# Routed attention and a gated layer on one core: later planned landings, a re-searched order, and code copies on GpSimd

## Chip, cores and metric

The kernel runs on one core of a Trainium2 chip. The metric is the device time of one execution in microseconds (us); the median of three runs of the kernel before is 307.97 us.

## What is computed

Attention in which a query sees only the keys of its own cluster, then a gated two-layer block. There are 4 batches, 8 heads, 768 positions and head size 64; 16 centroids for each head; the block takes 3072 rows of 512 to 2048 and back to 512.

```python
q_assign = argmax(einsum('bhsd,hcd->bhsc', q_n, c_n))      # nearest centroid of each query
k_assign = argmax(einsum('bhsd,hcd->bhsc', k_n, c_n))      # and of each key
mask = q_assign[:, :, :, None] == k_assign[:, :, None, :]
scores = where(mask, scale * q @ k.T, -1e9)
x = softmax(scores) @ v                                    # -> rows of 8 heads x 64
h = x @ w_in
out = (h * sigmoid(h)) @ w_out
```

## The kernel before

**One list of steps.** The kernel does not write out its order by hand. Each piece of work is a step with an engine, a cost, the steps it comes after, the buffers it uses and a key. `Plan.order` (a list scheduler) plays these costs through and returns all steps of all engines in one list, by planned start. The instructions are then emitted in that list's order: each engine gets its own in the order of the list, and waits at run time on semaphores. A planned time has no other effect on the chip than this order. Where the text below says that so much PE work stands "in the list" between two steps, it counts the matmuls that are emitted between them.

**How the plan treats a DMA.** A DMA step goes into one of three planned rings (SP, ACT, POOL). It is planned as landed when its transfer is through, plus a tail (`TURNED`, `EARLY` or `LAND`), plus the step's own `slack`. Steps that use the data are listed only after that. `lag` is the same for a step on an engine: the planned time from its end until another engine may use it.

**The stages, by line of the profile.** Batch 0 is prepared with TensorE transposes (L570, L615, L619, L877), and its attention runs in two rounds of query tiles. For batches 1 to 3 each pair of heads goes through this chain, twice (once for each head):

- SP loads k, q and v: L374, L389, L404. GpSimd makes the fp16 high part, L531, and VectorE the low part, L535. V is cast on GpSimd, L417.
- SP turns the twelve tiles of one head by a transposing DMA, `ab<-hl`, L550 (the step `turn_dma`).
- TensorE makes the centroid logits of the twelve tiles, L624 (12 small matmuls). VectorE sums and takes the maximum, L641 and L661; GpSimd subtracts, L673; VectorE marks the nearest centroid, L700 and L702, and transposes the marks in 32x32 blocks, L715 (`flip`).
- Four steps `put` copy the marks, one of four groups of 32 columns each, beside the turned tiles: three by GpSimd, L732, and the third by a small DMA on SP, L728. Which does which stands in the list `PUTB`.
- TensorE scores with 80 rows (64 of the head and 16 of the codes), L801; ScalarE exponentiates, L808; TensorE multiplies with v, L829; VectorE divides, L842 and L847. A pair of heads of x is turned by another transposing DMA, L866 (for the last pair by TensorE).

The gated block runs in nine units between the attention steps: three of two row tiles for batch 0, and two of three row tiles for each later batch. In a unit: first product, L907; tanh on ScalarE, L913; gate on VectorE, L918; second product, L942; the copy out of PSUM by ScalarE, L955, or VectorE, L957, as the list `EVAC` says for each unit; a store by SP, L960. The block's weights come in four and eight pieces by DMAs on GpSimd's queue, L976 and L980; before each of them a one-element copy from a buffer of attention, L974, holds the DMA back until that point.

**What sets the places.** `AT` holds planned start times of the attention of each round or batch, and `ML` of the nine units; both become keys. `SOON` says how many heads ahead loads and conversions may begin; `LEADS` by how much their key lies before the due time. SP has one in-order queue for loads, turned tiles, small code DMAs and stores.

```python
turned = [step("SP", 120 * n, turn_dma, after=[his, los], ..., load=195 * n, flip=True, slack=LATE)]
s_log = step("PE", SMALL * n * (2 if twin else 1), logits, after=[turned, s_cent, ...], ...)
placed.append(step(code_eng[g], w, put, after=[s_flip, s_log], use=[ohT, A], ...))
x = step("PE", mm_w(at), scores, after=[kdeps, qdeps], use=[A, sb], ...)
```

Of the kernel before, what the change touches and what calls it, by code (L numbers as in the profile page):

```python
# [198 lines left out]
def kernel(  # L199
# [84 lines left out]
    step = plan.step  # L284
# [16 lines left out]
    UNREAD = 80000.0  # L301
    COLD = 8500.0
    MORE = 250.0
    LATE = 600
    AT = [32.0, 63.0, 104.0, 133.9, 193.2, 273.6]
    ML = [55.5, 127.6, 75.5, 138.3, 182.4, 254.3, 222.5, 316.0, 335.3, 350.3]
    PUTB = ["POOL", "POOL", "SP", "POOL"]
    VC = ["ACT", "ACT", "POOL", "ACT"]
    VB = "POOL"
    TK = ["ACT", "ACT", "DVE", "DVE", "DVE"]  # L310
# [2 lines left out]
    TS = ["ACT", "DVE", "DVE", "DVE"]  # L313
    HI = ["ACT", "ACT", "ACT", "POOL"]
    HR = ["DVE", "POOL", "DVE", "POOL"]
    LEADS = [27.5, 133.1, 88.1]
    REST = [3, 6, 3, 11]
    RLOAD = [2, 0, 3, 0]
    SOON = [7, 4, 7, 4]
    XT = ["DVE", "ACT", "ACT", "DVE"]  # L320
    EVAC = ["DVE", "DVE", "DVE", "DVE", "DVE", "DVE", "DVE", "ACT", "ACT", "DVE"]
    SPARE = 0
    FINE = 2

# [149 lines left out]
    def part(b, p, segs, a0, due, lead=20.0, hi_eng="POOL", turn="DMA", twin=False, sub="POOL", code_eng=None, pace=None, wait=None):  # L474

        key = due - lead
        span = lead / 20.0
        n = sum(j1 - j0 for _, _, j0, j1 in segs)
# [67 lines left out]
        if turn == "DMA":  # L546

            def turn_dma():
                src = T["hl"][hl.i][:, 0 : n * pitch]
                nc.sync.dma_start_transpose(T["ab"][A.i][:, a0 : a0 + n, :], src)  # L550

            turned = [step("SP", 120 * n, turn_dma, after=[his, los], use=[hl, A], key=key + 2 * span, load=195 * n, flip=True, slack=LATE)]
        else:

            Z = buf("lt")
            chunks, where = [], {}
            for hh in sorted({h for _, h, _, _, _ in runs}):
                c = [t + i for _, h, j0, j1, t in runs if h == hh for i in range(j1 - j0)]
                if chunks and len(chunks[-1]) + len(c) <= 8:
                    chunks[-1] += c  # L560
                else:
                    chunks.append(c)
            for t in sum(chunks, []):
                where[t] = len(where)

            def turn_of(c, bank, c0, c1):
                def turn_pe():
                    pt = banks[bank.i].bitcast(f16)
                    for i, t in enumerate(c):
                        nc.tensor.transpose(  # L570
                            pt[0 : c1 - c0, i * 128 : (i + 1) * 128], tiles_of(hl)[:, t, c0:c1], ident
                        )

                return turn_pe

            def settle_of(c, bank, rows_, dst, eng):
                def settle():
                    pt = banks[bank.i].bitcast(f16)[0:rows_, 0 : len(c) * 128]
                    out_ = dst()[0:rows_, where[c[0]] : where[c[0]] + len(c), :].rearrange("p n c -> p (n c)")
                    if rows_ < 128 and eng == "ACT":  # L580
                        nc.scalar.activation(out=out_, in_=pt, func=AF.Copy, bias=0.0, scale=gain[0:rows_])
                    elif rows_ < 128:
                        nc.vector.tensor_scalar(out=out_, in0=pt, scalar1=gain[0:rows_], scalar2=None, op0=ALU.mult)  # L583
                    elif eng == "ACT":
                        nc.scalar.copy(out_, pt)
                    else:
                        nc.vector.tensor_copy(out_, pt)

                return settle

            def settle_w(c, eng):
                return act_w(128 * len(c)) + 60 if eng == "ACT" else dve_w(128 * len(c), 0.55, 40)

            turned = []
            for c in chunks:
                bank = buf("M")
                x = step("PE", 57 * len(c), turn_of(c, bank, 0, 128), after=[s_ident, his, los], use=[hl, bank], key=key + 2 * span)
                turned.append(
                    step(
                        turn[0], settle_w(c, turn[0]), settle_of(c, bank, 128, lambda: T["lt"][Z.i], turn[0]),  # L600
                        after=[x], use=[bank, Z], key=key + 3 * span,
                    )
                )
# [109 lines left out]
        if turn == "DMA":  # L713
            def flip():
                nc.vector.transpose(  # L715
                    T["ohT"][ohT.i][:, 0:n, :].rearrange("p n c -> p (n c)"),
                    T["oh"][oh.i][:, 0:n, :].rearrange("p n c -> p (n c)"),
                )

            s_flip = step("DVE", dve_w(32 * n, 1.04, 95), flip, after=marks, use=[oh, ohT], key=key + 12 * span)  # L720
            placed = []
            for g in range(4):

                def put(g=g):
                    dst = T["ab"][A.i][64 : 64 + HC, a0 : a0 + n, 32 * g : 32 * g + 32]
                    src = T["ohT"][ohT.i][32 * g : 32 * g + HC, 0:n, :]
                    if code_eng[g] == "SP":
                        nc.sync.dma_start(dst, src)  # L728
                    elif code_eng[g] == "ACT":
                        nc.scalar.copy(dst, src)  # L730
                    elif code_eng[g] == "POOL":
                        nc.gpsimd.tensor_copy(dst, src)  # L732
                    else:
                        nc.vector.tensor_copy(dst, src)

                w = {"ACT": 200 + act_w(32 * n) * 0.75, "POOL": pool_w(32 * n), "DVE": dve_w(32 * n, 0.08, 240), "SP": 600}[code_eng[g]]
                load = 10 * n if code_eng[g] == "SP" else None
                placed.append(step(code_eng[g], w, put, after=[s_flip, s_log], use=[ohT, A], key=key + 13 * span, load=load, port=code_eng[g] == "DVE"))

        else:  # L740
            last = {}
            for c in chunks:
                bank = buf("M")
                x = step("PE", 57 * len(c), turn_of(c, bank, D, HW), after=[marks, his, s_ident], use=[hl, bank], key=key + 12 * span)
                x = step(
                    turn[1], settle_w(c, turn[1]),
                    settle_of(c, bank, HW - D, lambda: T["ab"][A.i][:, a0 : a0 + n, :], turn[1]),
                    after=[x], use=[bank, A], key=key + 13 * span,
                )
                for t in c:  # L750
                    last[t] = x
# [10 lines left out]
    def attention(b, h, j0, j1, key, per, turn):  # L762
# [3 lines left out]
        nq = j1 - j0  # L766
# [96 lines left out]
        if turn == "DMA":  # L863

            def turn_x():
                nc.sync.dma_start_transpose(  # L866
                    T["xt"][X.i][:, p, cols].rearrange("p (n c) -> p n c", c=128),
                    T["xn"][xn.i][:, 0:nq, :].rearrange("p n c -> p (n c)"),
                )

            x = step("SP", 1240, turn_x, after=done, use=[xn, X], key=key + per - 3, load=195 * nq, flip=True, slack=LATE)
        else:
            bank = buf("M")

            def turn_x():
                for n in range(nq):
                    nc.tensor.transpose(banks[bank.i].bitcast(f16)[:, 128 * n : 128 * n + 128], T["xn"][xn.i][:, n, :], ident)  # L877

            def settle_x():
                dst, src = T["xt"][X.i][:, p, cols], banks[bank.i].bitcast(f16)[:, 0 : 128 * nq]  # L880
                if turn == "ACT":
                    nc.scalar.copy(dst, src)
                else:
                    nc.vector.tensor_copy(dst, src)

            x = step("PE", 57 * nq, turn_x, after=done, use=[xn, bank], key=key + per - 3)
            w = act_w(128 * nq) if turn == "ACT" else dve_w(128 * nq, 0.55, 40)
            x = step(turn, w, settle_x, after=[x], use=[bank, X], key=key + per - 3)
# [80 lines left out]
    def weight(kind, n, event):  # L969

        x, use, name = event

        def f():
            nc.gpsimd.tensor_copy(pace, T[name][use.i][:, D : D + 1])  # L974
            if kind == "in":
                nc.gpsimd.dma_start(  # L976
                    win_s[:, :, ts(n, 512)], moe_w_in.rearrange("(r p) f -> p r f", p=128)[:, :, ts(n, 512)]
                )
            else:
                nc.gpsimd.dma_start(  # L980
                    wout_s[:, 2 * n : 2 * n + 2, :],
                    moe_w_out[256 * n : 256 * n + 256, :].rearrange("(c p) d -> p c d", p=128),
                )

        return step("POOL", 840, f, after=[x], use=[use], key=-1, load=2450 if kind == "in" else 1220)


    want = {(n, h): AT[n] + (AT[n + 1] - AT[n]) * h / H for n in range(NU + B - 1) for h in range(H)}
# [104 lines left out]
```

## Time and profile before

| | |
|---|---|
| runs of the kernel before | 307.48, 307.97 and 308.44 us |
| the profiled execution | 307.14 us, of which the span from first to last instruction is 305.3 us |
| PE busy / idle in the span | 297.3 / 8.0 us |
| PE work that is never read (warm-up matmuls, L353, at the start) | 42 matmuls |
| granted TensorE clock, mean | 0.998 |
| transposing DMAs L550, issue to landing | 24, median 4.1 us |

The profile has a page and several views. The rows used below come from the page's table of engines; from the windows (busy time of each engine in a stretch, with the count of its instructions, the granted TensorE clock, the DMA engines' busy share and GB/s); from the timeline (start, length, engine, line, operation, and in square brackets the idle time before it and what ended it); from the waits (who waited for whom: us in total, times, longest); from the chain that ended last (start, length, what); and from the view of a single source line (shortest, median and longest duration in ns). A matmul's row lasts until the result has left the array, so matmuls overlap in the timeline; the time from one start to the next is what a matmul costs.

### The profile page before, as it was taken

Reading aid. Unit: us, or ns where it says so; the run is one execution under the profiler, and the core shown is the slowest. Engines: PE = TensorE matmul, PEld = TensorE weight load, DVE = VectorE, ACT = ScalarE, POOL = GpSimd, SP = SyncE. Lnnn points to the kernel's source line nnn. Section 1 sums busy time; section 2 is a strip of 40 time slices with the busy share of each in tenths; the row PEclk is TensorE's granted clock in tenths of the full one; section 3 lists DMA queues with packets and bytes.
Section 4 is the critical chain, followed back from the end, with each engine's and each line's share of the span. In section 5 each row is a group of like instructions: output and inputs, shape, how many; then the busy total and the mean of one; then the engine's idle time right before and its main releaser. Section 6 shows DMA issues by size and latency. Waiting matters only on the chain.

```text
span 305.3 us, 8425 instructions
## 1 busy us (share of the span) xinstructions
PE 297.3 (97%) x3257; PEld 196.1 (64%) x3257; DVE 207.9 (68%) x493; ACT 223.7 (73%) x461; POOL 108.2 (35%) x218
## 2 busy tenths in 40 slices
PE   8999999999999999999999998999999999999995
PEld 6898777577677746666656765665655565554644
DVE  5999688778869955989766997867562323750820
ACT  5869999888988838999777998778782380642721
POOL 2546432656466480717564563733000000000000
PEclk9999999999999999999999999999999999999999
DMA  7999969993969888486969848472010201002001
GB/s 245 290 249 251 206 104 224 103 248 87 226 100 237 191 167 196 138 156 162 237 149 223 155 154 169 131 129 66 0 37 36 84 12 71 35 0 73 32 34 69
DMA packets 73688, 41.82 MB, mean 137 GB/s; under 512 B 53041, under 2 KB 70705, under 8 KB 73649
## 3 DMA queue, kind: packets, MB, share of 16 engines
q1 hardware_dynamic: 68944, 36.94, 51.4%
q0 software_dynamic: 4288, 4.20, 8.6%
q8 instruction: 25, 0.41, 0.6%
q10 hardware_dynamic: 416, 0.16, 0.2%
q14 instruction: 15, 0.11, 0.1%
HBM read 27.30 MB, written 6.29 MB: 110 GB/s over the span
## 4 chain that ended last, share of the span: by engine, by line
PE 80%; DMA 7%; ACT 5%; DVE 3%; issue 1%; POOL 1%; SPq 0%; ACTq 0%; POOLq 0%
PE bank L942 27%; PE bank L907 22%; PE bank L801 16%; PE bank L829 9%; ACT P L808 4%; DMA ab<-hl 3%; PE bank L570 3%; DMA wout_s<-in_moe_w_out_dram 2%; PE bank L624 2%; DMA nk<-in_k_dram 2%; POOL hl L531 1%; PE bank L615 1%; DVE hl L535 1%; DVE gq L918 1%; PE bank L619 1%
## 5 line engine op out<-in xcount | busy, mean ns | idle before, releaser
L808 ACT ACTIVATE P<-bank 128x512 f16<-128x512 f32 x288 | 157.8, 640 | 30.8 <-PE bank L801 29.1
L942 PE MATMUL bank<-wout_s,gq 128*128 128x512 f16 (+1 forms) x400 | 97.1, 370 | 0.4 <-DMA wout_s<-in_moe_w_out_dram 0.4
L907 PE MATMUL bank<-xt,win_s 128*128 128x384 f16 (+1 forms) x576 | 95.6, 308 | 0.0
L918 DVE SCALAR_TENSOR_TENSOR gq<-tn,bank 128x384 f16<-128x384 f32 (+1 forms) x144 | 70.1, 504 | 32.4 <-ACT tn L913 28.7
L801 PE MATMUL bank<-ab 80*128 80x256 f16 (+1 forms) x384 | 90.9, 326 | 0.0
L913 ACT ACTIVATE tn<-bank 128x384 f32<-128x384 f32 (+1 forms) x144 | 67.8, 488 | 24.1 <-PE bank L907 20.9
L907 PEld LDWEIGHTS <-win_s 128*128 128x128 f16 x576 | 55.0, 97 | 28.8
L942 PEld LDWEIGHTS <-gq 128*128 128x128 f16 x400 | 37.9, 98 | 33.1 <-issue 0.7
L829 PEld LDWEIGHTS <-P 128*128 128x128 f16 x1152 | 45.6, 97 | 11.9 <-ACT P L808 0.8
L829 PE MATMUL bank<-vt,P 128*128 128x65 f16 x1152 | 49.8, 193 | 0.7 <-ACT P L808 0.6
L732 POOL COPY ab<-ohT 16x384 f16<-16x384 f16 x72 | 39.3, 546 | 28.2 <-DVE ohT L715 11.7
L801 PEld LDWEIGHTS <-ab 80*128 80x128 f16 x384 | 34.6, 97 | 20.7 <-DVE ab L583 0.2
L673 POOL TENSOR_TENSOR Df<-L,mx 128x192 f32<-128x192 f32 x24 | 12.3, 511 | 41.9 <-DVE mx L661 39.7
L957 DVE COPY ot<-bank 128x512 f32<-128x512 f32 x18 | 12.3, 681 | 16.4 <-PE bank L942 15.6
L535 DVE SCALAR_TENSOR_TENSOR hl<-nk,hl 128x384 f16<-128x384 f32 (+1 forms) x29 | 19.8, 687 | 3.3 <-POOL hl L531 3.1
L535 DVE SCALAR_TENSOR_TENSOR hl<-nq,hl 128x384 f16<-128x384 f32 (+3 forms) x33 | 20.9, 635 | 0.6 <-POOL hl L531 0.3
L641 DVE TENSOR_REDUCE L<-bank 128x192 f32<-128x384 f32 x24 | 13.3, 552 | 10.0 <-PE bank L624 9.7
L847 DVE TENSOR_TENSOR xn<-bank,rz 128x384 f16<-128x384 f32 (+2 forms) x40 | 19.1, 477 | 1.4 <-DVE rz L842 0.2
L531 POOL TENSOR_SCALAR hl<-nk 128x384 f16<-128x384 f32 (+1 forms) x25 | 13.6, 547 | 7.6 <-PE bank L570 6.7
L955 ACT COPY ot<-bank 128x512 f32<-128x512 f32 (+1 forms) x7 | 3.7, 524 | 17.2 <-PE bank L942 17.2
L531 POOL TENSOR_SCALAR hl<-nq 128x384 f16<-128x384 f32 (+2 forms) x27 | 15.2, 566 | 1.7 <-DMA nq<-in_q_dram 1.1
L417 POOL CAST vt<-nv 128x384 f16<-128x384 f32 x26 | 14.6, 582 | 1.1 <-DMA nv<-in_v_dram 0.7
(60 smaller groups left out, 183.6 us busy)
## 6 DMA issues: line engine op xcount, KB each, us to landing
nv<-in_v_dram SPq DMA_DIRECT2D x16, 384.0 KB, 5.6
out_dram<-ot SPq DMA_DIRECT2D x23, 256.0 KB, 2.3
nk<-in_k_dram SPq DMA_DIRECT2D x15, 384.0 KB, 4.3
nq<-in_q_dram SPq DMA_DIRECT2D x12, 384.0 KB, 4.7
wout_s<-in_moe_w_out_dram POOLq DMA_DIRECT2D x8, 256.0 KB, 7.2
win_s<-in_moe_w_in_dram POOLq DMA_DIRECT2D x4, 512.0 KB, 9.3
nq<-in_q_dram SPq DMA_DIRECT2D x4, 256.0 KB, 6.5
nk<-in_k_dram SPq DMA_DIRECT2D x2, 192.0 KB, 2.8
```

What stands on the lines that cost most here:

```text
L417: (nc.gpsimd if eng == "POOL" else nc.vector).tensor_copy(dst, src)
L531: nc.gpsimd.tensor_scalar(out=dh, in0=src, scalar1=qs, scalar2=1.0, op0=ALU.mult, op1=ALU.mult)
L535: nc.vector.scalar_tensor_tensor(out=dl, in0=src, scalar=qs, in1=dh, op0=ALU.mult, op1=ALU.subtract)
L732: nc.gpsimd.tensor_copy(dst, src)
L801: nc.tensor.matmul(banks[sb.i][:, at : at + 128 * (c1 - c0)], ab[0:80, kt[j], :], ab[0:80, qt + c0 : qt + c1, :].rearrange("p n c -> p (n ...
L808: nc.scalar.activation(out=T["P"][P.i][:, 0:at], in_=banks[sb.i][:, 0:at], func=AF.Exp, bias=0.0, scale=ESC if b else -ESC)
L829: nc.tensor.matmul(banks[O.i][:, (D + 1) * t : (D + 1) * t + nn], w, vt[:, VW * j : VW * j + nn], start=(j == 0), stop=(j == NJ - 1), skip ...
L847: nc.vector.tensor_tensor(out=T["xn"][xn.i][:, 0:nq, (h % 2) * D : (h % 2) * D + D], in0=banks[O.i][:, 0 : (D + 1) * nq].rearrange("p (t c ...
L907: nc.tensor.matmul(banks[bank.i][:, 0:n], win_s[:, r, ts(fb, 128)], T["xt"][xtb[b].i][:, r, 128 * j0 : 128 * j1], start=(r == 0), stop=(r ...
L913: nc.scalar.activation(out=T["tn"][tn.i][:, 0:n], in_=banks[bank.i][:, 0:n], func=AF.Tanh, bias=0.0, scale=1.0)
L918: nc.vector.scalar_tensor_tensor(out=T["gq"][g.i][:, fb % 4, 0:n], in0=T["tn"][tn.i][:, 0:n], scalar=1.0, in1=banks[bank.i][:, 0:n], op0=A ...
L942: nc.tensor.matmul(banks[bank.i][:, 0 : c1 - c0], T["gq"][gqs[fc // 4].i][:, fc % 4, ts(t, 128)], wout_s[:, fc, c0:c1], start=(fc == 0), s ...
```

## The change

It changes planning constants, and four engine assignments. No instruction's work is changed.

```diff
-    LATE = 600
-    AT = [32.0, 63.0, 104.0, 133.9, 193.2, 273.6]
-    ML = [55.5, 127.6, 75.5, 138.3, 182.4, 254.3, 222.5, 316.0, 335.3, 350.3]
-    PUTB = ["POOL", "POOL", "SP", "POOL"]
+    LATE = 900
+    FLIP = 1500
+    DONE = 600
+    WSL = 1000
+    AT = [32.0, 63.0, 91.3, 118.4, 233.2, 272.8]
+    ML = [55.5, 113.0, 73.2, 121.1, 198.2, 239.3, 267.5, 305.4, 257.3, 449.1]
+    PUTB = ["POOL", "POOL", "POOL", "POOL"]
-    LEADS = [27.5, 133.1, 88.1]
+    LEADS = [27.5, 133.1, 361.9]
-    SOON = [7, 4, 7, 4]
+    SOON = [7, 5, 7, 4]
-    EVAC = ["DVE", "DVE", "DVE", "DVE", "DVE", "DVE", "DVE", "ACT", "ACT", "DVE"]
+    EVAC = ["DVE", "DVE", "DVE", "ACT", "ACT", "ACT", "DVE", "ACT", "ACT", "ACT"]
-            turned = [step("SP", 120 * n, turn_dma, ..., flip=True, slack=LATE)]
+            turned = [step("SP", 120 * n, turn_dma, ..., flip=True, slack=FLIP)]
-                placed.append(step(code_eng[g], w, put, ..., port=code_eng[g] == "DVE"))
+                placed.append(step(code_eng[g], w, put, ..., port=code_eng[g] == "DVE", lag=Plan.LAG.get(code_eng[g], 0) + DONE))
-            x = step("SP", 1240, turn_x, ..., flip=True, slack=LATE)
+            x = step("SP", 1240, turn_x, ..., flip=True, slack=FLIP)
-        return step("POOL", 840, f, after=[x], use=[use], key=-1, load=2450 if kind == "in" else 1220)
+        return step("POOL", 840, f, after=[x], use=[use], key=-1, load=2450 if kind == "in" else 1220, slack=WSL)
```

`LATE` stays the slack of the k, q and v loads of batches 1 to 3; `FLIP` is the slack of both kinds of transposing DMA; `DONE` is added to the lag of the code copies; `WSL` is the slack of the weight pieces. Of `EVAC` the first nine entries are used. So the third code copy moves from SP's queue to GpSimd, 24 times, and the copies out of PSUM of units 3 to 5, nine in all, move from VectorE to ScalarE.

The order of every engine is the same up to the late part of batch 0's attention: on PE the first 530 matmuls of 3257, with all 42 warm-up matmuls, stand as they stood. Behind that all engines are re-ordered. PE has the same 3257 matmuls of the same shapes.

More of the change, by code (lines that the diff above doesn't have):

```diff
@@ L550, in turn_dma @@
                 nc.sync.dma_start_transpose(T["ab"][A.i][:, a0 : a0 + n, :], src)
-            turned = [step("SP", 120 * n, turn_dma, after=[his, los], use=[hl, A], key=key + 2 * span, load=195 * n, flip=True, slack=LATE)]
+            turned = [step("SP", 120 * n, turn_dma, after=[his, los], use=[hl, A], key=key + 2 * span, load=195 * n, flip=True, slack=FLIP)]
         else:
@@ L737, in part @@
                 load = 10 * n if code_eng[g] == "SP" else None
-                placed.append(step(code_eng[g], w, put, after=[s_flip, s_log], use=[ohT, A], key=key + 13 * span, load=load, port=code_eng[g] == "DVE"))
+                placed.append(step(code_eng[g], w, put, after=[s_flip, s_log], use=[ohT, A], key=key + 13 * span, load=load, port=code_eng[g] == "DVE", lag=Plan.LAG.get(code_eng[g], 0) + DONE))
         else:
@@ L869, in turn_x @@
                 )
[L871 removed]
+            x = step("SP", 1240, turn_x, after=done, use=[xn, X], key=key + per - 3, load=195 * nq, flip=True, slack=FLIP)
         else:
```

## The prediction

> **What bounds the kernel now.** First the page's head, then the busy time by stretch.
>
> ```profile
> span 305.3 us, 8425 instructions
> PE 297.3 (97%) x3257; PEld 196.1 (64%) x3257; DVE 207.9 (68%) x493; ACT 223.7 (73%) x461; POOL 108.2 (35%) x218
> ...
> 30.00:50.00 20.00, 19.94 (x284) 15.46 (x281) 15.17 (x43) 19.75 (x48) 7.38 (x15) 1.00 0.94 167
> 50.00:60.00 10.00, 9.61 (x132) 5.84 (x130) 8.17 (x20) 8.70 (x19) 5.30 (x11) 1.00 1.09 159
> 60.00:70.00 10.00, 9.87 (x114) 7.36 (x113) 7.67 (x22) 8.91 (x21) 5.29 (x11) 1.00 0.97 218
> 70.00:120.00 50.00, 50.00 (x588) 33.91 (x586) 38.59 (x95) 39.85 (x88) 26.66 (x50) 1.00 0.81 170
> 120.00:140.00 20.00, 19.62 (x243) 13.25 (x242) 17.77 (x41) 18.73 (x41) 9.96 (x19) 1.00 0.74 180
> 140.00:180.00 40.00, 40.00 (x472) 25.72 (x471) 31.03 (x73) 34.64 (x70) 23.11 (x43) 1.00 0.82 183
> 180.00:200.00 20.00, 19.06 (x220) 12.22 (x219) 16.55 (x36) 17.31 (x35) 12.46 (x23) 1.00 0.62 126
> 200.00:300.00 100.00, 100.00 (x726) 56.59 (x725) 46.80 (x91) 52.11 (x105) 4.02 (x8) 1.00 0.15 46
> ```
>
> PE bounds it: 97% busy, at a granted clock (third number from the end) of 1.00. A busy PE can still be a slow one, so I take its cost by starts, from the chain of waits.
>
> ```profile
> 30.46 0.45 PE bank L570 x8
> 56.19 0.65 PE bank L801 x3
> 66.19 4.81 PE bank L907 x44
> 85.59 1.09 PE bank L829 x36
> 105.45 0.29 PE bank L624 x12
> 108.30 6.91 PE bank L942 x32
> 137.76 0.65 PE bank L907 x4
> ```
>
> That is 0.45 us for eight TensorE transposes, 0.217 for a unit of scores (512 columns), 0.44 or 0.65 for a step of the first product (four matmuls of 256 or 384 columns), 0.18 for a step with v (six matmuls), 0.3 for a step of logits and 0.43 for a step of the second product (two matmuls). They run back to back; the change keeps all of them. It can win only where PE waits. Behind 30 us the stretches show 0.06 + 0.39 + 0.13 + 0.38 + 0.94 = 1.90 us of idle PE, and none behind 200 us. Who is waited for, and the longest case:
>
> ```profile
> PEld L624 <- DMA ab<-hl: 3.5, 6, 1.2
> PE bank L624 <- DMA ab<-hl: 1.3, 2, 0.9
> PE bank L942 <- DMA wout_s<-in_moe_w_out_dram: 0.4, 1, 0.4
> ...
> 187.45 0.38 PE L801 MATMUL bank<-ab 80*128 80x512 f16 x1
> 188.77 0.47 PE L624 MATMUL bank<-stk,ab 128*128 128x32 f16 x12 [0.94 <-DMA ab<-hl]
> ...
> 46.37 7.59 DMA wout_s<-in_moe_w_out_dram
> 131.69 5.33 DMA ab<-hl
> 183.53 5.20 DMA ab<-hl
> ```
>
> The score matmul that starts at 187.45 costs 0.217, yet the logits start only at 188.77: 1.10 us are lost, of which the view calls 0.94 idle and shows 0.16 as the matmul's drain. Each wait is thus 0.16 longer than its idle time: five visible ones make 1.90 + 0.80 = 2.7 us, and some waits on turned tiles short enough to vanish in the drain (the view counts six) may add 0.3. So **about 3.0 us** is the most that a new order can win; all but some 0.25 of it waits for a DMA, of a turned tile or of a weight piece.
>
> **The later landings.** They move no data; they make the list put more PE work between a DMA and its user. In the old list there stood, between the turning DMA at 183.53 and its logits, 6 score units, 3 first-product steps and 5 steps with v: 1.30 + 1.95 + 0.90 = 4.15 us. The DMA took 5.20: short by 1.05, as seen (1.10). The DMA at 131.69 had 5 score units, 3 first-product steps, 6 steps with v and one of logits, 4.4 us, against 5.33. Over all 24:
>
> ```profile
> L550 SPq DMA_TRANSPOSE ab<-hl x24: 1294/1461/5414, 44.4 to 200.2; - x24
> DMA to landing us min/median/max: 3.7/4.1/10.2
> ```
>
> Counted in the same way, 21 of the 24 had 4.0 to 5.6 us in the old list. In the new one none has under 4.99 (6 score units, 4 first-product steps, 6 with v). There are three kinds.
>
> (a) Thirteen that follow no load closely have 4.99 to 7.1 us. Against the median 4.1 nothing is lost; against 5.33 the tightest lose 0.3 each. Bounds 0 and 1.4 in all; I take 0.2, near the median's end.
>
> (b) Nine stand right behind a k, q and v load on SP, 1.0 to 2.3 us after the v load. Their room is 7.48, 7.26, 7.37, 7.8, 8.58, 7.89, 6.87, 7.54 and 8.68 us (the shortest: 8 first-product steps, 6 score units, 2 steps with v). In the old order such a place is held by the smaller turning DMA of x; these are two SP issues and the landing of the second:
>
> ```profile
> 92.05 0.47 SPq L404 DMA_DIRECT2D nv<-in_v_dram  x1
> 93.03 1.24 SPq L866 DMA_TRANSPOSE xt<-xn  x1
> ...
> DMA to landing us min/median/max: 5.0/5.0/5.0
> ```
>
> The DMA of x has six tiles, not twelve; I take 6 us for the larger one, which fits all nine rooms, and charge 0.25 for a bad case. The bounds are 3.7 (nothing lost) and 10.2, the longest row, which would cost 22 us in all.
>
> (c) The first two, for batch 1, now stand behind a k and a q load, with 8.7 and 9.8 us of room. The 10.2 us case is of this spot in the old order:
>
> ```profile
> 46.70 0.57 SPq L389 DMA_DIRECT2D nq<-in_q_dram  x1
> 47.37 0.42 SPq L404 DMA_DIRECT2D nv<-in_v_dram  x1
> 47.89 5.41 SPq L550 DMA_TRANSPOSE ab<-hl  x1
> ```
>
> There SP was held for 5.41 us behind q and v. Now one load less stands between (v follows), but k comes close ahead. Bounds: no loss, or 10.2 - 8.7 = 1.5; I take 0.3.
>
> **Weight pieces.** The last one took 7.59 us from its issue and stopped PE for 0.39 + 0.16 = 0.55. From its step to its first user the list had 6.0 us and now has 6.8 (three more score units and eight transposes, one step of logits less): 0.8 more than covers 0.55. Bounds 0 and 0.9 (if it now meets k and q); I take 0.1.
>
> **Code copies.** 24 of these move from SP to GpSimd:
>
> ```profile
> L732 POOL COPY ab<-ohT x72: 496/500/891, 56.2 to 209.9; 16x384 f16<-16x384 f16 x72
> L728 SPq DMA_DIRECT2D ab<-ohT x24: 591/610/1939, 55.6 to 208.7; - x24
> L702 DVE TENSOR_SCALAR oh<-Df x24: 198/210/546, 54.2 to 207.6; 128x96 f16<-128x96 f32 x24
> ...
> L715 DVE STREAM_TRANSPOSE ohT<-oh 128x384 f16<-128x384 f16 x24 | 13.9, 578 | 0.8
> L641 DVE TENSOR_REDUCE L<-bank 128x192 f32<-128x384 f32 x24 | 13.3, 552 | 10.0 <-PE bank L624 9.7
> L673 POOL TENSOR_TENSOR Df<-L,mx 128x192 f32<-128x192 f32 x24 | 12.3, 511 | 41.9 <-DVE mx L661 39.7
> ...
> SPq L728 <- DVE ohT L715: 23.3, 15, 3.4
> ```
>
> GpSimd gets 24 x 0.50 = 12 us on its 108, in a stretch (50 to 210 us) where it was about 55% busy. SP loses 24 issues of 0.61, 15 of which first waited for VectorE's marks, 23.3 us in all, with loads and turned tiles queued behind. Four copies in a row take 2.0 us instead of three beside a DMA. From logits to scores stand seven short operations before them, none longer than the 0.58 of L715, so the chain is at most 7 x 0.58 + 2.0 = 6.1 us; the tightest room in the new list, for batch 1's first two heads, is 9.3. Even four copies at 0.891, 7.6 us, fit. If that cover were gone, each head would wait 0.5.
>
> The mark L702 takes 210 ns mostly and up to 546 ns, so VectorE can be held up. From 50 to 200 us it is idle for a fifth of the time (the third column above), which covers more such marks: 0, and at worst 24 x (0.546 - 0.198) = 8.4 us of VectorE's time against 30 idle. The Trainium skill, SBUF — State Buffer, section Terms, has a rule against more GpSimd copies: the two engines share a port pair under an exclusive lock, and the loser waits for the whole instruction. The trace agrees, 0.35 us being most of a copy. By that rule VectorE could lose 24 x 0.5 = 12 us, an estimate; by the row's median nearly nothing.
>
> **Output copies.** Nine go from VectorE to ScalarE. From 140 to 220 us of PE work the new list gives ScalarE these nine and 93 exponentials and 32 tanh, where the old gave 90 and 44: twelve more of one sort, twelve fewer of the other, where it was busy for 34.64 of 40 us. It is full only at 30 to 50 us (19.75 of 20), where PE's small wait of 0.06 + 0.16 stands; the new list has two exponentials more there and five fewer in the 10 us behind. I keep 0.2; bounds 0 and 0.7. In the old list no load or turned head stands behind 203 us, in the new one none either; the last seven copies stay on ScalarE, and the tail costs what it did.
>
> **Sum.** Remaining waits: 0.2 + 0.25 + 0.3 + 0.1 + 0.2 = 1.05 instead of 3.0, a gain of 1.95. The profiled execution took 307.14 (1.84 outside its span), so 305.2 against itself. It was 0.83 faster than the median of the runs, 307.97; the gain taken from the median gives 306.0. Some of what slower runs lose must be late DMAs too, which the same room covers, so I say **305.8 us**.
>
> **The rivals.**
>
> *Slower: turned tiles behind three loads.* One mechanism, kind (b): SP's queue works the loads off first, so nine turned tiles land later than they did. If they land halfway between my 6 and 10.2, at 8.1 us, the nine lose 0.62 + 0.84 + 0.73 + 0.3 + 0 + 0.21 + 1.23 + 0.56 + 0 = 4.5 us, and the time is 305.8 + 4.5 - 0.25 = 310.0. It decides from a landing of about 7.75 us on, where the nine lose 2.2 and the gain is gone. For it: the 10.2 row. Against: the 5.0 row, and that weight traffic, which shared the engines at 47 us, is over by then. The Trainium skill, DMA: Bandwidth & Descriptors, section Queues, rings and completion order, says that on each DMA engine a ring's descriptors are consumed in order; the 5.41 us issue agrees.
>
> *No change: the waits only move.* The first two turned tiles lose 1.5, the last weight piece 0.9 and ScalarE's full stretch 0.7, all at 40 to 60 us: 3.1 us, as much as was won, 307.7. For it: that spot holds the longest landings of the trace. Against: the room there grew by 2.8 us for the first tile and 0.8 for the weights.
>
> *All waits go.* 307.76 (mean of the four executions) - 3.0 = 304.8.
>
> **How the numbers follow.** Forecast 0.68, slower rival 0.09, no change 0.11, all waits gone 0.12. A difference of 0.3% (0.9 us) is about what can be told from none. Faster: 0.68 + 0.12 and a little of the third, 0.81; same 0.10; slower 0.09. The range runs from just under 304.8 to the third case, 304.6 to 307.8; the slower rival is left outside.
>
> **What would show it.** Right: the waits of L624 on turned tiles fall from 4.8 us in two rows to under 1; no wait of L942 on weights; PE idle behind 30 us under 0.7; turned tiles behind loads landing in 5 to 7 us; VectorE's L535 and L702 little slower. Wrong: a new row of PE waiting for `ab<-hl` with a case over 1 us, landings over 7.75, scores (L801) waiting for GpSimd's copies, or PE's spacing by starts changed.

## The result and the profile after

The changed kernel takes 304.8 us (median of nine runs, 304.0 to 306.24) where the kernel before, run beside it, takes 307.48 (nine runs, 306.31 to 308.44). The ratio is 0.9921 with a 95% interval of 0.9898 to 0.9945. A second set of six runs of the same kernel gave 305.07 and 0.9925 (0.9904 to 0.9947). The forecast was 305.8 in a range of 304.6 to 307.8, and faster as the likeliest sign.

The profiled execution took 305.28 us. These are the page's head and the windows of the changed kernel; its line numbers are 3 higher than before (logits L627, scores L804, second product L945).

```profile
span 303.5 us, 8340 instructions
PE 297.6 (98%) x3257; PEld 196.9 (65%) x3257; DVE 196.6 (65%) x484; ACT 226.2 (75%) x470; POOL 118.7 (39%) x242
```
```profile
30.00:50.00 20.00, 20.00 (x271) 15.11 (x267) 14.97 (x41) 19.74 (x48) 7.67 (x15) 1.00 0.97 177
50.00:60.00 10.00, 10.00 (x153) 6.65 (x152) 7.87 (x24) 10.00 (x22) 4.35 (x8) 1.00 1.12 171
60.00:70.00 10.00, 10.00 (x102) 6.22 (x101) 8.01 (x19) 5.68 (x13) 8.92 (x17) 1.00 0.65 186
70.00:120.00 50.00, 49.30 (x597) 34.93 (x596) 37.51 (x98) 39.64 (x93) 31.09 (x60) 1.00 0.83 179
120.00:140.00 20.00, 20.00 (x246) 13.60 (x245) 16.42 (x40) 18.33 (x40) 11.68 (x23) 1.00 0.60 146
140.00:180.00 40.00, 40.00 (x421) 24.62 (x419) 28.53 (x66) 32.19 (x64) 21.95 (x42) 1.00 0.74 174
180.00:200.00 20.00, 20.00 (x200) 12.06 (x199) 10.00 (x25) 16.32 (x32) 7.31 (x16) 1.00 0.75 152
```

PE's busy time is what it was (297.6 against 297.3), and its idle time behind 30 us is 0.70 us instead of 1.90, all of it in one stretch (from 200 to 300 us PE is busy throughout, as before). Both cases in that stretch are before logits. The timeline of PE (and of VectorE, for the first case) shows them, and the chain that ended last names the DMA of the second:

```profile
97.23 0.60 PE L945 MATMUL bank<-wout_s,gq 128*128 128x512 f16 x2
97.96 0.45 PE L627 MATMUL bank<-stk,ab 128*128 128x32 f16 x12
...
107.73 1.67 PE L945 MATMUL bank<-wout_s,gq 128*128 128x512 f16 x7
109.98 0.47 PE L627 MATMUL bank<-stk,ab 128*128 128x32 f16 x12 [0.57 <-DMA ab<-hl]
```
```profile
97.25 0.65 DVE L960 COPY ot<-bank 128x512 f32<-128x512 f32 x1
```
```profile
102.06 7.87 DMA ab<-hl
```

Seven matmuls of 0.217 from 107.73 are through at 109.25, and the logits start at 109.98: 0.73 us are lost to a turned tile that landed 7.87 us after its issue. At 97.23 two such matmuls end at 97.66, the logits start at 97.96, as soon as VectorE's copy out of PSUM is through (97.90): 0.29. The chain that ended last puts this copy right ahead of these logits.

**One way of counting for all kernels.** I add up, from the starts of PE's matmuls, every place where the next one comes more than 25 ns later than the last one's usual cost. I begin with the 531st matmul, the first whose place the change moves. (The expectations below count from 28 us, which adds 0.1 to 0.2 for some transposes of batch 0.) Before: 3.04 us, of it 2.26 on turned tiles (1.10, 0.54, 0.29, 0.16, 0.14, 0.03), 0.55 on a weight piece, 0.23 on ScalarE. After: 1.30, the two cases above and 0.28 in short ones. In a second profile of the changed kernel: 0.86.

| kernel | profiled time | waits of PE by starts | start of the 531st matmul | rest |
|---|---|---|---|---|
| before | 307.14 | 3.04 | 32.31 | 271.79 |
| changed | 305.28 | 1.30 | 32.48 | 271.50 |
| changed, second profile | 305.46 | 0.86 | 33.10 | 271.50 |

"Rest" is the time less the two columns before it; over all fourteen profiled executions of this study (thirteen kernels) it stayed between 271.37 and 272.06. So these waits account for the differences: of the 1.86 us between the first two rows they are 1.74. The third column shows why one pair of profiles says less than the medians. The 531st matmul starts between 32.06 and 33.55 us, without a relation to the change, and both profiles of the changed kernel lie above its medians while that of the kernel before lies below its own.

**The turned tiles did not land sooner.** The view of the transposing DMA's line, changed kernel:

```profile
L553 SPq DMA_TRANSPOSE ab<-hl x24: 1273/1748/4344, 44.7 to 211.5; - x24
DMA to landing us min/median/max: 3.7/4.3/8.6
```

The median is 4.3 us, before it was 4.1. What grew is the time between the landing and the first logits' start, from a median of 0.9 us to 1.76. That is room in the list.

### The profile page after: what moved, and what is told of

The parts are those of the page before. It is cut to its first block, busy times and chain, and to the rows that moved or that the text cites. A ratio compares the mean times of both kernels' runs of the same rounds, so it can differ in the third digit from the quotient of the medians.

```text
span 303.5 us, 8340 instructions
## 1 busy us (share of the span) xinstructions
PE 297.6 (98%) x3257; PEld 196.9 (65%) x3257; DVE 196.6 (65%) x484; ACT 226.2 (75%) x470; POOL 118.7 (39%) x242
## 4 chain that ended last, share of the span: by engine, by line
PE 94%; DMA 3%; ACT 1%; DVE 0%; issue 0%; ACTq 0%
PE bank L910 27%; PE bank L945 26%; PE bank L804 19%; PE bank L832 11%; PE bank L573 3%; DMA ab<-hl 3%; PE bank L627 2%; PE bank L356 2%; ACT P L811 1%; PE bank L618 1%; PE bank L622 1%; PE bank L880 1%; ACT lt L588 0%; DVE ot L960 0%; ACT ot L958 0%
## 5 line engine op out<-in xcount | busy, mean ns | idle before, releaser
L811 ACT ACTIVATE P<-bank 128x512 f16<-128x512 f32 x288 | 160.2, 650 | 25.7 <-PE bank L804 24.6
L945 PE MATMUL bank<-wout_s,gq 128*128 128x512 f16 (+1 forms) x400 | 100.2, 370 | 0.0
L910 PE MATMUL bank<-xt,win_s 128*128 128x384 f16 (+1 forms) x576 | 96.8, 308 | 0.0
L804 PE MATMUL bank<-ab 80*128 80x256 f16 (+1 forms) x384 | 92.8, 326 | 0.0
L735 POOL COPY ab<-ohT 16x384 f16<-16x384 f16 x96 | 51.5, 536 | 27.6 <-DVE ohT L718 13.5
L945 PEld LDWEIGHTS <-gq 128*128 128x128 f16 x400 | 37.3, 98 | 30.4
L804 PEld LDWEIGHTS <-ab 80*128 80x128 f16 x384 | 35.0, 97 | 21.9 <-issue 0.2
L958 ACT COPY ot<-bank 128x512 f32<-128x512 f32 (+1 forms) x16 | 8.9, 558 | 18.0 <-PE bank L945 17.9
L538 DVE SCALAR_TENSOR_TENSOR hl<-nq,hl 128x384 f16<-128x384 f32 (+3 forms) x33 | 19.9, 602 | 0.9 <-POOL hl L534 0.9
L845 DVE RECIPROCAL rz<-bank 128x6 f32<-128x6 f32 (+2 forms) x40 | 7.2, 180 | 17.1 <-PE bank L832 9.7
L534 POOL TENSOR_SCALAR hl<-nq 128x384 f16<-128x384 f32 (+2 forms) x27 | 14.1, 524 | 1.5 <-DMA nq<-in_q_dram 1.4
L718 DVE STREAM_TRANSPOSE ohT<-oh 128x384 f16<-128x384 f16 x24 | 13.8, 576 | 0.8
```

The lines of the kernel that those rows point to most:

```text
L534: nc.gpsimd.tensor_scalar(out=dh, in0=src, scalar1=qs, scalar2=1.0, op0=ALU.mult, op1=ALU.mult)
L538: nc.vector.scalar_tensor_tensor(out=dl, in0=src, scalar=qs, in1=dh, op0=ALU.mult, op1=ALU.subtract)
L718: nc.vector.transpose(T["ohT"][ohT.i][:, 0:n, :].rearrange("p n c -> p (n c)"), T["oh"][oh.i][:, 0:n, :].rearrange("p n c -> p (n c)"),)
L804: nc.tensor.matmul(banks[sb.i][:, at : at + 128 * (c1 - c0)], ab[0:80, kt[j], :], ab[0:80, qt + c0 : qt + c1, :].rearrange("p n c -> p (n ...
L811: nc.scalar.activation(out=T["P"][P.i][:, 0:at], in_=banks[sb.i][:, 0:at], func=AF.Exp, bias=0.0, scale=ESC if b else -ESC)
L910: nc.tensor.matmul(banks[bank.i][:, 0:n], win_s[:, r, ts(fb, 128)], T["xt"][xtb[b].i][:, r, 128 * j0 : 128 * j1], start=(r == 0), stop=(r ...
```

## The experiments

The theory is that the gain is this room alone, won by planning the landing later, and that the rest of the change (copies on GpSimd, the new targets, the output copies) carries or costs little. Its first rival says that the code copies or the new order did it. I tried the parts in both kernels. Each kernel's ratio is to the kernel before, run beside it on the same chip. The line numbers in the rows shown are up to three higher than in the kernel before.

**1. Old list, the logits and what follows them moved 0.9 us later.** `chains` holds, for each head that SP turns, the steps from the logits to the code copies; the two lines that fill it are left out here ("...").

```diff
+    ...
-    for s in plan.order():
+    todo_ = plan.order()
+    for c in chains:
+        for s in [*c[:-1], *c[-1]]:
+            s.start += 900
+    for s in sorted(todo_, key=lambda s: (s.start, s.n)):
```

> The old list, with one edit: of each of the 24 heads of batches 1 to 3 the logits and all that follows them up to the code copies are emitted 0.9 us later among the other steps; the rest, the code copy on SP among it, stays. Theory (the gain is room between a turning DMA and its logits): the waits of PE on turned tiles, 2.3 us in the profile before (1.10, 0.54, 0.29, 0.16, 0.14, 0.03), shrink by 0.9 each to some 0.2; PE waits behind 28 us fall from 3.1 to about 1.1, and the time by 1.5 to 2.0 us, ratio about 0.994. Rival (the gain is the new search of targets, or the code copies): under 0.5 us of change, waits on turned tiles still 2 us or more.

Measured 310.68 us, ratio 1.0089 (1.0055 to 1.0123): slower. Rows of its waits, then VectorE and PE at one place:

```profile
PEld L879 <- DVE xn L849: 2.1, 3, 0.8
...
PE bank L625 <- DMA ab<-hl: 1.0, 1, 1.0
PE bank L803 <- DMA ab<-ohT: 1.0, 1, 1.0
```
```profile
86.70 0.56 DVE L716 STREAM_TRANSPOSE ohT<-oh 128x384 f16<-128x384 f16 x1
87.19 0.51 DVE L536 SCALAR_TENSOR_TENSOR hl<-nk,hl 128x384 f16<-128x384 f32 x1
87.63 1.07 DVE L920 SCALAR_TENSOR_TENSOR gq<-tn,bank 128x256 f16<-128x256 f32 x3
```
```profile
87.27 0.59 PE L944 MATMUL bank<-wout_s,gq 128*128 128x512 f16 x2
88.09 1.44 PE L803 MATMUL bank<-ab 80*128 80x512 f16 x7 [0.23 <-DVE gq L920]
```

The tiles' cases fell from six to one (1.19 us). But VectorE works in the order of the list: steps moved back by 0.9 us now stand in front of gates and divisions that PE wants, here a block transpose ahead of the gates L920. Such waits for VectorE are 2.6 us in all, a code DMA is late by 1.16, and PE waits 5.73. Pushed into this finished list, the room cost more than it won. The theory, as I had put it, was wrong here.

**2. Old list, the third code copy on GpSimd instead of SP.** The place in the list stays.

```diff
                     if code_eng[g] == "SP":
-                        nc.sync.dma_start(dst, src)
+                        nc.gpsimd.tensor_copy(dst, src)
```

> The old list, with the third code copy done by GpSimd at the place of the list where SP issued its DMA. Theory: the room of the turned tiles is the same, their landing hardly so; PE waits on turned tiles stay over 1.5 us, time within 0.7 us of before. Rival (the small DMAs on SP delay the turned tiles): landings get shorter by 0.5 us or more, the waits go, 1.5 to 2 us faster.

Measured 310.32 us, 1.0069 (1.0044 to 1.0094): slower. From its waits:

```profile
DVE hl L535 <- POOL hl L531: 8.0, 9, 1.8
PEld L624 <- DMA ab<-hl: 6.5, 8, 2.0
PE bank L624 <- DMA ab<-hl: 3.8, 5, 1.5
```

and the first of these rows in the kernel before:

```profile
DVE hl L535 <- POOL hl L531: 3.4, 5, 1.3
```

The copies themselves stop nothing. But GpSimd also makes the fp16 high parts, L531. They now come later, VectorE's low parts wait 8.0 us for them instead of 3.4, the turning DMAs are issued later, and seven tiles cost PE 5.02 us. I had expected no more than 0.7 us of loss. Late issues are not all of it: all seven had less PE work between issue and logits than before (0.3 to 1.1 us less), but four also landed later than before, among them the costliest (1.63 us lost; 5.3 us from issue to landing, before 4.0). So the change's copies are no gain by themselves; in this list, which has no room for them, they are a loss.

**3. Changed list, the third code copy back on SP.**

```diff
-                    if code_eng[g] == "SP":
+                    if code_eng[g] == "SP" or g == 2:
```

> The new list, with the third code copy done by a DMA on SP at its place, as in the kernel before. Theory: the room is larger than what the 24 small DMAs add; PE waits behind 28 us rise from 1.5 by under 0.7, time under 0.8 us over the changed kernel. Rival (the copies carry the gain): back to 3 us of waits, 1.5 to 2 us slower than the changed kernel.

Measured 309.7 us, 1.0059 (1.0025 to 1.0093) (profiled execution 307.86). SP's queue and then PE in the timeline, and the windows around the place:

```profile
58.11 1.14 SPq L377 DMA_DIRECT2D nk<-in_k_dram  x1
...
60.38 1.19 SPq L869 DMA_TRANSPOSE xt<-xn  x1
61.68 0.75 SPq L731 DMA_DIRECT2D ab<-ohT  x1
```
```profile
63.85 0.18 PE L627 MATMUL bank<-stk,ab 128*128 128x32 f16 x1
65.56 2.57 PE L804 MATMUL bank<-ab 80*128 80x512 f16 x12 [1.54 <-DMA ab<-ohT]
67.92 1.06 PE L945 MATMUL bank<-wout_s,gq 128*128 128x512 f16 x2
68.78 1.06 PE L804 MATMUL bank<-ab 80*128 80x512 f16 x2
```
```profile
63.50:67.00 3.50, 1.96 (x23) 1.25 (x21) 2.92 (x9) 0.96 (x2) 2.69 (x6) 1.00 0.57 158
67.00:70.50 3.50, 3.50 (x12) 1.33 (x10) 1.51 (x3) 3.50 (x9) 3.27 (x6) 0.51 0.25 46
70.50:74.00 3.50, 3.50 (x28) 2.55 (x27) 1.62 (x4) 2.33 (x7) 1.98 (x5) 1.00 1.05 256
```

The new list has no room for a DMA between the marks and the scores: here it stands behind k, q, v and a turned x, and PE waits 1.69 us by starts. What came behind I had not reckoned with: the granted clock is 0.51 for 3.5 us, and the matmuls stand 0.43 us apart instead of 0.217, which costs 1.68 us more. With 0.44 at a second such place, PE's waits are 4.10. So the change's copies on GpSimd are needed in its own list. By the ratios that is over 4 us above the changed kernel; neither the theory (under 0.8) nor the rival (1.5 to 2) had such a loss. The median lies 1.8 us above the profiled execution, and the mean granted clock that each execution has on record points at more such falls: 307.5 to 309.0 us at 0.998 and 0.999, 307.9 to 309.7 at 0.993 and 0.994 (the profiled one, with one fall, is of these), 309.7 to 312.2 at 0.989. One fall of 3.4 us to half takes 0.0056 off the mean. But only one execution was profiled, so the further falls aren't shown.

**4. Changed list, the logits and what follows them 0.9 us sooner**, with the lines of experiment 1 and `s.start -= 900`.

> The new list, with the logits of each head and what follows them up to the code copies emitted 0.9 us sooner; all else stays. Theory: in the profile of the changed kernel a turned tile landed 0.7 us late in one case, 0.05 and 0.27 early in two and 0.9 to 1.2 early in four; with 0.9 less, PE waits on turned tiles rise from 0.7 to about 2.2 us, time 1.2 to 1.8 us over the changed kernel. Rival (the search of targets or the copies carry the gain): under 0.5 us.

Measured 306.37 us, 0.995 (0.9919 to 0.9981). PE waits 1.90: 0.41 on a tile, and 0.43, 0.37 and 0.27 at VectorE's and ScalarE's work. By the ratios that is 0.9 us over the changed kernel, with overlapping intervals. The theory missed here too: I had expected 2.2 us of waits on tiles. At run time the logits stood only 0.3 us closer behind the landings than in the changed kernel (medians 1.47 and 1.76 us), and the tile that had landed 7.87 us after its issue there took 6.07 here. So this run says little on the room, for or against.

**5. The kernel before with one constant: 1500 instead of 600 as the slack of both transposing DMAs, and planned anew.** Nothing else of the change.

```diff
+    FLIP = 1500
-            turned = [step("SP", 120 * n, turn_dma, ..., flip=True, slack=LATE)]
+            turned = [step("SP", 120 * n, turn_dma, ..., flip=True, slack=FLIP)]
-            x = step("SP", 1240, turn_x, ..., flip=True, slack=LATE)
+            x = step("SP", 1240, turn_x, ..., flip=True, slack=FLIP)
```

> The kernel before with one constant: the slack of both kinds of transposing DMA 1500 instead of 600, and the list planned again from that; targets, code copy on SP, weights and output copies as before. The room between a turning DMA and its logits is then 4.76 to 10.3 us (before 3.99 to 9.5, 21 of 24 under 5.7). Theory (the gain is this room, when the whole list is planned for it): PE waits on turned tiles fall under 1 us, waits behind 28 us from 3.1 to 1.2 to 2.0, time 1.0 to 2.0 us faster than before. Rival (the search of targets or the code copies carry the gain): within 0.7 us of before, or slower.

Measured 305.65 us, 0.9936 (0.9909 to 0.9963). PE waits 1.10, of them on a tile 0.12. Two stretches of its windows, and the view of its turning line:

```profile
120.00:140.00 20.00, 20.00 (x246) 13.49 (x244) 17.24 (x43) 18.95 (x42) 9.28 (x18) 1.00 0.86 200
...
180.00:200.00 20.00, 20.00 (x226) 12.73 (x223) 16.99 (x39) 17.77 (x37) 11.97 (x22) 1.00 0.76 143
```
```profile
DMA to landing us min/median/max: 3.7/4.0/9.8
```

The idle PE of the kernel before at 120 to 140 and at 180 to 200 us (0.38 and 0.94) is gone, with the third code copy still on SP and with the old targets. The DMAs were about as slow as before; but the two that cost most before (5.33 and 5.20 us) landed in 4.0 and 3.9 us here, so I crossed the two profiles. A tile's room is the PE work between its DMA's issue and its logits at run time, waits left out; the tile loses the time by which its landing, and 0.05 us from there to the logits, is longer. Tile by tile, with the landings of the kernel before, the rooms of the kernel before lose 2.83 us (the wait on a weight piece hid 0.55 of it) and those of this list 0.23. With the landings of this run they lose 2.77 and 0.13. So it is the rooms, not faster DMAs.

This one constant gives 0.0064 of the change's 0.0079, and the two intervals overlap. Part of what is missing lies outside the span from first to last instruction: there each of the ten executions spends about 2.2 us, where those of all other kernels spend 1.7 to 1.9. By the spans alone the ratio is 0.9922, and that of the changed kernel's second set 0.9923. Where the 0.4 us come from is open.

**6 and 7. The two halves of the change crossed.** Six: all slacks and the copies on GpSimd, with the old `AT`, `ML`, `LEADS`, `SOON` and `EVAC` (lines not shown). Seven: all of the change but the slacks:

```diff
-    LATE = 900
-    FLIP = 1500
-    DONE = 600
-    WSL = 1000
+    LATE = 600
+    FLIP = 600
+    DONE = 0
+    WSL = 0
```

> All of the change but the search: new slacks, all code copies on GpSimd, but AT, ML, LEADS, SOON and EVAC of before. Room of the turned tiles 4.77 us or more, of the last weight piece 6.35 (before 6.0, changed 6.8). Theory: nearly the changed kernel, PE waits behind 28 us 1.3 to 2.0, time 1.2 to 2.5 us faster than before. Rival (the search carries it): within 0.7 us of before, or slower.

> The changed kernel's targets, copies and output copies, but the old slacks (600 for loads and turned tiles, none added for code copies and weights), planned again. Room of the turned tiles from 3.8 us, 12 of 24 under 4.6. Theory: turned tiles land late again, PE waits on them over 1.5 us, time 1.5 to 3 us over the changed kernel, that is within 1 us of before. Rival (the search carries the gain): within 0.7 us of the changed kernel, ratio to before 0.994 or less.

Six: 306.19 us, 0.9948 (0.992 to 0.9976). No tile is waited for, but a weight piece costs 0.95 (the landing itself 0.8 in its waits) and many short waits for engines make up 2.43 in all.

```profile
PE bank L945 <- DMA wout_s<-in_moe_w_out_dram: 0.8, 1, 0.8
```

Seven: 306.64 us, 0.9965 (0.9937 to 0.9993). Two tiles are late again, by 0.93 and 0.39, and two waits for VectorE are 0.47 and 0.38; 3.10 in all. So the slacks take away nearly all of the tiles' waits under either set of targets. That the searched targets take away what the slacks and the copies disturb elsewhere fits the 2.43 against 1.30 and 0.86, but the intervals of six and of the changed kernel overlap. And seven is 1.0 us faster than before by the medians, though its profile has as much waiting (3.10 against 3.04): what it wins there isn't seen.

**8. Changed list, the output copies of units 3 to 5 on VectorE again.**

```diff
+            by = "DVE" if (b, j0) in ((1, 0), (1, 3), (2, 0)) else eng
-            def leave(bank=bank, ot=ot, eng=eng, w=c1 - c0):
+            def leave(bank=bank, ot=ot, eng=by, w=c1 - c0):
```

> The changed kernel with its list as it is, but the nine output copies of units 3 to 5 done by VectorE instead of ScalarE, as before. Theory: 9 x 0.6 us on VectorE where it is idle a fifth of the time or more; PE waits within 0.5 us, time within 0.7 us of the changed kernel. Rival (ScalarE taking them is part of the gain): over 1 us slower than the changed kernel.

Measured 305.69 us, 0.993 (0.9906 to 0.9953), against 0.9921 and 0.9925 with the copies on ScalarE: no difference that can be told. Two tiles were late (0.50, 1.01): the first is the late one of the changed kernel, the second landed 5.9 us after its issue where that of the changed kernel took 3.8. Why it did is open.

**9 to 11. More room.** Nine is the changed kernel once more, for the noise. Ten is the changed kernel with `FLIP = 2400`, eleven experiment 5 with 2100.

> The changed kernel as it is, for a second profile and for times beside the next three. Theory: ratio to before 0.990 to 0.995; PE waits behind 28 us 1.0 to 2.2 us, the tightest turned tiles the only DMA waited for. Rival (the first profile was a lucky one): over 2.5 us of waits, ratio over 0.996.

> The changed kernel with the slack of the transposing DMAs at 2400 instead of 1500, planned again. Room of the turned tiles 5.66 to 10.9 us (changed 4.99 to 9.8), 8.1 instead of 7.4 where one landed 0.7 late. Theory: no wait on a turned tile over 0.2 us; time 0 to 1 us under the changed kernel, if ScalarE and VectorE keep up, as their work between PE's places, counted in the list, says. Rival (more room is paid for in another queue): waits on VectorE or ScalarE over 1 us, time over the changed kernel.

> As e5, the kernel before with the slack of the transposing DMAs alone, but 2100 instead of 1500; targets not searched for it. Room of the turned tiles at least 5.5 us. But the list now gives ScalarE up to 1.9 us more work than PE's work beside it takes, at two places (about 116 and 197 us of PE work). Theory: no wait on turned tiles, but 1 to 3.5 us of new waits on ScalarE; slower than e5 by 1 us or more. Rival (room is all that counts): as fast as e5 or faster.

Nine gave the second set of runs above. Ten: 305.72 us, 0.9946 (0.9931 to 0.9962). Every tile lands 1.56 us or more before its logits, and PE waits only 0.77, but the time is no better than the changed kernel's, of which I had expected up to 1 us less. Eleven: 310.59 us, 1.009 (1.0069 to 1.011), with no tile waited for. Its windows at the two places where it loses:

```profile
110.00:126.00 16.00, 15.42 (x142) 8.54 (x141) 7.26 (x15) 13.20 (x28) 5.58 (x11) 1.00 0.70 158
198.00:212.00 14.00, 13.15 (x150) 7.91 (x149) 10.15 (x22) 12.52 (x28) 8.12 (x15) 1.00 0.54 135
```

and the kernel before in the same stretches:

```profile
110.00:126.00 16.00, 16.00 (x173) 9.80 (x171) 10.08 (x22) 9.98 (x20) 7.87 (x15) 1.00 0.68 164
198.00:212.00 14.00, 14.00 (x131) 8.50 (x130) 10.49 (x24) 11.10 (x21) 5.64 (x11) 1.00 0.54 104
```

With more slack the plan pushed heads together: ScalarE has 28 instructions where it had 20 and 21, and PE stands 0.27 us at a time before scores, whose PSUM banks the exponentials have not freed. It waits 5.64 us. A later landing is thus not free: it moves which work lies beside which. That 1500 under the old targets did not meet this is luck as far as these runs show.

**12. The kernel before with all code copies on GpSimd, planned anew.**

```diff
-    PUTB = ["POOL", "POOL", "SP", "POOL"]
+    PUTB = ["POOL", "POOL", "POOL", "POOL"]
```

> The kernel before with all four code copies on GpSimd and nothing else, planned again with the old slacks. Room of the turned tiles 3.78 us or more, 14 of 24 under 4.4 (before 9). Theory: moving the copies gives nothing by itself; PE waits on turned tiles 2 us or more, time from 0.7 us faster to 2 us slower than before. Rival (with a list planned for it, the copies carry part of the gain): 0.8 us faster or more.

Measured 307.5 us, 1.001 (0.999 to 1.003): no change. Its waits of logits:

```profile
PEld L624 <- DMA ab<-hl: 3.8, 7, 0.9
PE bank L624 <- DMA ab<-hl: 1.6, 4, 0.6
```

Six tiles cost 2.71 us by starts, about what they cost before (2.26). Planned for, the copies on GpSimd neither win nor lose.

## Why the prediction was right, step by step

**What bounds it, and what can be won.** Right. PE's 3257 matmuls cost what they did, and I took 3.0 us as the most that a new order can win; by starts the waits were 3.04. That the gain is room between a turning DMA and its logits is shown by experiment 5, which adds hardly anything but room, by the crossing of rooms and landings there, and by 12, which moves the copies without adding room and wins nothing. Experiment 7, which takes the room away, shows it in part: tiles are waited for again (1.32 us) and the waits are as long as before, but 1.0 us of the gain stays.

**(a) Tiles behind no load**, taken at 0.2: 0, with some luck. The tightest of them landed 0.27 us before its logits in the first profile, 5.2 us after its issue, with 4.8 us of PE work between: it was in time only because PE had stood still for 0.73 us for the tile before it.

**(b) Tiles behind k, q and v**, taken at 0.25 with a landing of 6 us: one case, 0.73, in the second profile 0.23. The nine landed 6.5, 6.6, 7.9, 4.0, 6.0, 5.3, 4.3, 4.4 and 5.3 us after their issue, a mean of 5.6. The size was near and the spread wider than my "5 to 7". The third is also the slower rival in small: SP's queue at that place in the changed kernel.

```profile
99.51 0.47 SPq L377 DMA_DIRECT2D nk<-in_k_dram  x1
...
101.47 0.47 SPq L407 DMA_DIRECT2D nv<-in_v_dram  x1
102.06 4.34 SPq L553 DMA_TRANSPOSE ab<-hl  x1
```

SP is held for 4.34 us in the issue behind three loads, and the tile lands past the 7.75 us from which that rival decides. One of nine did so; the rival needed all nine.

**(c) The first two tiles**, taken at 0.3: 0. The first had the longest landing of all, 8.6 us, and was still 1.4 us early.

**Weight pieces**, taken at 0.1: 0, and 0.34 in the second profile. Experiment 6, with the same slack of 1000 under the old targets, lost 0.95 there, so the planned slack doesn't secure it. **ScalarE's full stretch**, taken at 0.2: about 0.2 in both.

**Code copies**, taken at 0 with a cover of 9.3 us of room: right, with these views of their line and of VectorE's marks in the changed kernel.

```profile
L735 POOL COPY ab<-ohT x96: 496/500/892, 60.3 to 221.8; 16x384 f16<-16x384 f16 x96
```
```profile
L705 DVE TENSOR_SCALAR oh<-Df x24: 169/206/416, 59.1 to 219.0; 128x96 f16<-128x96 f32 x24
```

24 more copies at 0.50 us, and GpSimd is busy for 10.5 us more (I had 12). The marks' longest case is 0.416 us where it was 0.546, and three of the 24 take over 0.25 us where seven did, so by this row VectorE is held up no more often than before; of the 12 us that the Trainium skill's rule on the shared port pair (SBUF — State Buffer, section Terms) would allow, nothing is seen. What I missed is what stands behind a copy on GpSimd: the fp16 conversions, on which the next turning DMA depends. Experiment 2 shows that price, 2.8 us more waits of PE than before, when the list isn't planned for it.

**Output copies**, taken at 0: right in size (experiment 8). One wait of 0.29 was not in my sum: logits waiting for a PSUM bank that VectorE's copy L960 still read.

**The sum.** I had 1.05 us of waits left; measured were 1.30 and 0.86. The mechanism holds. That the sum came so near is partly luck: in the first profile (a), (c) and the weights, 0.6 of it, cost nothing, while one tile of (b) cost 0.5 more than its term and some 0.4 came from waits that are not in it, the 0.29 above all.

The forecast lies 0.7 to 1.0 us above the medians. About 0.5 of that is the base: I counted from 307.97, the median of three executions, and the medians beside the changed kernel were 307.48 and 307.43. The rest is the gain: from the median I forecast 2.2, and 2.7 and 2.4 came. I argued that executions longer than the profiled one lose more on late DMAs; this isn't shown, since none of them was profiled.

**The signs I had named** did not all come out. Waits for turned tiles fell, but in the views of the first profile to 1.7 us in two rows, not under 1:

```profile
PEld L627 <- DMA ab<-hl: 1.1, 1, 1.1
PE bank L627 <- DMA ab<-hl: 0.6, 1, 0.6
```

PE's idle time is 0.70, not under it, and the second profile waits for a weight piece. Two landings, 7.9 and 8.6 us, are over the 7.75 that I named as a sign of being wrong. That bound was worked out for all nine tiles of (b) at once; a single landing past it decides nothing, and the sign should have said so. No score waits for a copy of GpSimd, and PE's spacing is unchanged.

**Open.** Whether the search and the copies on GpSimd add anything to experiment 5's one constant: 0.9936 against 0.9921 and 0.9925, with overlapping intervals, and no difference by the spans. `WSL` and `DONE` were not tried alone. No version tried beats the changed kernel.

## What to carry to other kernels

Where one engine is busy for 97% and nearly all of its few waits are for DMAs, compare for each DMA the work that the list puts between its issue and its user with the landing times in the trace, not with their median: here 4.0 to 5.6 us of room for 21 of 24 against landings of 3.7 to 5.3 us cost 2.3 us, and 0.9 us more of planned landing won nearly all of it. Let the planner place that room, and measure how much: 1.5 us more than before (experiment 11) lost 0.9%. Shifting steps in a finished list, or moving copies to another engine at their old place, lost 0.7 to 0.9% as well. When an engine takes over a copy, look first at what else it makes and who waits for that.

## What the chip showed unexpectedly

A single wait can cost twice. In experiment 3 PE stood idle for 1.54 us, went on at a granted clock of 1.00, and some 1.5 us later fell to 0.51 for 3.5 us, which cost as much again (1.68 after 1.69). In experiment 2 waits of nearly that size, with 1.47 and 1.29 us of idle time, were followed by a clock of 1.00. The Trainium skill, TensorE: Matmul & The Clock Gate, Part 1 on the HAM clock gate, puts the fall to half rate after an idle window of about 3.4 us, the return to full rate after a busy one of that length, and says that the window runs freely. The half rate and its length (0.50 for 3.41 us by the trace's clock records) agree; the idle time here was less than half of that.

The traces say more on what was different. In all fourteen the clock changes only in whole steps of 3.41 us: the stretches at full rate last 18, 69, 87, 88 or 89 of them. Here is the step ahead of the fall, and the two steps of experiment 2 that hold its two waits:

```profile
63.66:67.07 3.41, 1.87 (x22) 1.16 (x21) 2.90 (x8) 1.03 (x3) 2.60 (x6) 1.00 0.54 146
```
```profile
79.33:82.74 3.41, 1.94 (x27) 1.07 (x26) 1.62 (x5) 1.23 (x4) 1.84 (x4) 1.00 0.99 317
137.36:140.77 3.41, 2.12 (x39) 1.34 (x36) 2.54 (x8) 2.11 (x5) 1.02 (x3) 1.00 1.01 275
```

PE was busy for 1.87 us in the first and for 1.94 and 2.12 in the others, and no step at full rate in the fourteen profiles, their ends left out, has less than the first. So it may be the busy time in such a step that counts, and not the length of one wait. With a single fall ahead of the end this isn't shown, and 0.07 us is a small difference.
